# Windowed attention and its feed-forward layer: a lower place in the schedule for the weights' conversion passes while attention runs alone

## The chip, the cores and the metric

The kernel runs on one core of one Trainium2 chip. The metric is the device time in microseconds (us) of one execution, as the median of several runs. In the text PE is the matrix engine, DVE the vector engine, ACT the scalar engine, POOL the general-purpose engine, and SP the engine whose queue issues nearly all DMA transfers. Each engine works through a queue of its own in order: an instruction whose input is late holds up everything behind it in that queue.

## What is computed

Attention over 8 batches and 8 heads of width 64, with 32 global and 512 local positions; a local query sees the 32 global keys and the local keys within 32 positions. Its output, 4352 rows of 512 numbers, goes through two matrix products with an ELU between them.

```python
s_ll = np.where(np.abs(pos[:, None] - pos[None, :]) <= 32, scale * q_l @ k_l.T, -1e9)
out_l = sm(concat([scale * q_l @ k_g.T, s_ll])) @ concat([v_g, v_l])
out_g = sm(scale * q_g @ concat([k_g, k_l]).T) @ concat([v_g, v_l])
x = concat([out_g, out_l]).transpose(0, 2, 1, 3).reshape(8 * 544, 512)
h = x @ w_in                                   # w_in: 512 x 2048, float64 in the inputs
g = np.where(h > 0, h, np.exp(np.minimum(h, 0)) - 1)
out = g @ w_out                                # w_out: 2048 x 512, float64 in the inputs
```

## The kernel before

**The weights.** `w_in` and `w_out` arrive as 8-byte floats, are loaded as pairs of 32-bit integers, and have to become two float16 tensors each, a high and a low part. This is done in 16 units, alternately of `w_in` (m = 0) and `w_out` (m = 1), each a tile of 128 x 1024 elements. One unit is a chain of steps:

- `s0`: absolute value on ACT (L188) and a clamp on POOL (L189).
- `s1a`, `s1b`, `s1c`: three integer passes on DVE (L193, L196, L200) that put a 32-bit float together; L196 and L200 read two tiles.
- `s1d`: the largest magnitude, on DVE (L205) for m = 0 and on ACT (L207) for m = 1.
- `s2`: for m = 0 a transpose on PE (L141) and a reduction on DVE (L142), so that all partitions know the maximum.
- `s3`: three one-column operations on DVE (L131, L132, L136) and the high part on ACT (L216).
- `s4`: the low part on DVE (L219), which also reads two tiles.

Two tiles `raw` hold the loaded integers, three tiles `cu` the work. The DMA that loads the next unit but one therefore waits on SP until the last reader of its `raw` tile (L200 or L207) is done.

**Attention.** It goes through slots, each of four steps of the outer loop; in the stretch that matters here a slot is one tile of 128 queries for four heads, or the global queries of four heads. `stage_s` multiplies queries by keys on PE (L772) and masks and takes the minimum on DVE (L783); `ex` is the exponential on ACT (L789); `norm` takes the sum's reciprocal on DVE (L793, L794), scales on POOL (L796) and on DVE (L798). `stage_t` transposes on PE (L812) and copies on DVE (L814); `stage_u` transposes the global parts on PE (L745 to L748) and copies them on ACT (L749, L751, L753) and, for one tile in four, on DVE (L756). `stage_v` multiplies by the values on PE (L856, L825), copies on ACT (L862), and adds up on DVE (L867 to L871). `stage_ga` does the global queries (PE L706, DVE L718, L719, ACT L723). Transposes of a tile come two slots after its scores, its product with the values three slots after.

**The order.** Two things set it. The program issues instructions in an order that the Python loops fix: `defer(n, fn)` puts a step n ticks later, and one tick passes for each attention step while attention runs alone, which it does for its first 66 steps (`lead[0]` is true). Units 0 to 4 begin at steps 1, 8, 18, 30 and 64. From step 66 on the feed-forward layer's matmuls (L327, L450, later L485) are issued between attention's steps and fill PE. The second thing is a scheduler that runs at compile time: it goes through all instructions, estimates when each has its inputs, and gives each engine, of those that it takes to be ready, the one with the lowest number. The number is the place in the program's order. `tc.high_priority(offset=-BEHIND)`, with BEHIND = 60, gives what is issued inside it a number higher by 60. What the scheduler has put in a queue stays so on the chip, whatever is ready first there. `tc.keep_in_program_order` (on L193 and on the transposes of L141) pins an instruction behind the one that the program issued before it on the same engine, and says nothing of those after.

The kernel has a function `behind` for this already, inside `add_up`, which prepares sums of the weights after all are converted.

Of the kernel before, what the change touches and what calls it, by code (L numbers as in the profile page):

```python
# [44 lines left out]
BEHIND = 60  # L45
# [15 lines left out]
def attn_ffn(ctx: ExitStack, tc: tile.TileContext, qT, qgT, kT, vT, vgT, vpT, w_in, w_out, mask, out):  # L61
# [23 lines left out]
    def defer(n, fn):  # L85
        if n == 0:
            return fn()
        later.setdefault(now[0] + n, []).append(fn)

    def tick():  # L90
        now[0] += 1
        for fn in later.pop(now[0], []):
            fn()

    def drain():
        while later:
            tick()

    lead = [True]

# [27 lines left out]
    def power(dst, src):  # L128

        dst = dst.bitcast(I32)  # L130
        nc.vector.tensor_scalar(dst, src.bitcast(I32), 0x7f800000, None, ALU.bitwise_and)  # L131
        nc.vector.tensor_scalar_max(dst, dst, LOW)  # L132

    def inverse(dst, src):

        nc.vector.tensor_scalar(dst.bitcast(I32), src.bitcast(I32), TOP, -1.0, ALU.subtract, ALU.mult)  # L136

    def all_max(dst, src):

        tp = ps_a.tile([P, 512], F32, name="pa")  # L140
        tc.keep_in_program_order(nc.tensor.transpose(tp[:, 0:P], src.to_broadcast([P, P]), ident))  # L141
        nc.vector.tensor_reduce(out=dst, in_=tp[:, 0:P], op=ALU.max, axis=AX.X)  # L142
# [15 lines left out]
    def load_weights():  # L158
        todo = [(group, m, p) for group in "abcd" for p in range(*GROUPS[group]) for m in range(2)]
        raws = [fetch(*todo[0][1:])]  # L160
        yield
        for n, (group, m, p) in enumerate(todo):
            if n + 1 < len(todo):
                raws.append(fetch(*todo[n + 1][1:]))
            unit(m, p, raws[n])
            if (m, p) == (1, GROUPS[group][1] - 1):
                defer(12, lambda group=group: tables(group))
                if p == NP - 1:
                    defer(13, lambda: tables("f"))
            yield  # L170
# [6 lines left out]
    def unit(m, p, raw):  # L177
        f = slice(2 * p * P, 2 * (p + 1) * P)
        shape = [P, NC, 2 * P] if m == 0 else [P, 2, DM]
        parts = [w[:, :, f] for w in win] if m == 0 else [w[:, 2 * p:2 * p + 2, :] for w in wout]  # L180
        pw = (pww if m == 0 else pwo)[:, p:p + 1]
        u = ffn.tile(shape, F32, name="cu", bufs=3)
        mx = ffn.tile([P, 4], F32, name="cm", bufs=4)
        high, low = raw[..., 1], raw[..., 0]
        ui = u.bitcast(I32)

        def s0():
            nc.scalar.activation(u, high.bitcast(F32), AF.Abs)  # L188
            nc.gpsimd.tensor_scalar(u, u, FMAX, FMIN, ALU.min, ALU.max)  # L189

        def s1a():
            tc.keep_in_program_order(
                nc.vector.tensor_scalar(ui, ui, 3, 0x3ffffff8, ALU.logical_shift_left, ALU.bitwise_and))  # L193

        def s1b():
            nc.vector.scalar_tensor_tensor(out=ui, in0=high, scalar=-0x40000000, in1=ui,  # L196
                                           op0=ALU.bitwise_and, op1=ALU.bitwise_or)

        def s1c():
            nc.vector.scalar_tensor_tensor(out=ui, in0=low, scalar=29, in1=ui,  # L200
                                           op0=ALU.logical_shift_right, op1=ALU.bitwise_or)

        def s1d():
            if m == 0:
                nc.vector.tensor_reduce(out=mx[:, 0:1], in_=u, op=ALU.max, axis=AX.XY, apply_absolute_value=True)  # L205
            else:
                nc.scalar.activation(low.bitcast(F32), u, AF.Abs, accum_out=mx[:, 1:2])  # L207

        def s2():
            if m == 0:  # L210
                all_max(mx[:, 1:2], mx[:, 0:1])

        def s3():
            power(pw, mx[:, 1:2])
            inverse(mx[:, 3:4], pw)
            nc.scalar.activation(parts[0], u, AF.Copy, scale=mx[:, 3:4])  # L216

        def s4():
            nc.vector.scalar_tensor_tensor(out=parts[1].rearrange("p a b -> p (a b)") if m else parts[1],  # L219
                                           in0=u.rearrange("p a b -> p (a b)") if m else u, scalar=mx[:, 3:4],  # L220
                                           in1=parts[0].rearrange("p a b -> p (a b)") if m else parts[0],
                                           op0=ALU.mult, op1=ALU.subtract)

        d = 1 if lead[0] else 2
        lag = 7 if m else 16
        for i, fn in ((1, s0), (1 + d, s1a), (1 + 2 * d, s1b), (1 + 3 * d, s1c), (1 + 4 * d, s1d),
                      (1 + lag, s2), (2 + lag, s3), (3 + lag, s4)):
            defer(i, fn)

    def tables(group):  # L230

# [30 lines left out]
    def add_up(p, cross):  # L262


        if not sums:
            sums["rows"] = [ffn.tile([P, NP * 512], F16, name="raw") for _ in range(2)]
            sums["diag"] = [ffn.tile([P, NP * 256], F16, name="cu", bufs=3) for _ in range(2)]
        w = ffn.tile([P, 2, DM], F32, name="cu", bufs=3)
        s = ffn.tile([P, 512], F32, name="tmp", bufs=3)
        d = None if cross else ffn.tile([P, 512], F32, name="tmp", bufs=3)[:, 0:256]  # L270
        pr = slice(2 * p, 2 * p + 2)
        flat = [a[:, pr, :].rearrange("p a b -> p (a b)")[:, 256:768] for a in wout]
        rows = [a[:, p * 512:(p + 1) * 512] for a in sums["rows"]]
        diag = [a[:, p * 256:(p + 1) * 256] for a in sums["diag"]]
        todo = ((flat, s),) if cross else ((rows, s), (diag, d))

        def s0():
            nc.vector.tensor_add(w, wout[0][:, pr, :], wout[1][:, pr, :])  # L278

        def s1():  # L280
            if cross:
                nc.vector.tensor_sub(s, w[:, 1, :], w[:, 0, :])
            else:
                nc.vector.tensor_add(s.rearrange("p (a b) -> p a b", a=2), w[:, :, 0:256], w[:, :, 256:512])
                nc.vector.tensor_add(d, w[:, 0, 0:256], w[:, 1, 256:512])

        def s2():
            for dst, src in todo:
                nc.scalar.copy(dst[0], src)

        def s3():
            for dst, src in todo:
                nc.vector.tensor_sub(dst[1], src, dst[0])
            if cross:
                added.append(p)

        def behind(fn):
            with tc.high_priority(offset=-BEHIND):
                fn()

        for i, fn in enumerate((s0, s1, s2, s3)):
            defer(1 + 2 * i, lambda fn=fn: behind(fn))
# [6 lines left out]
    def ffn_stream():  # L309
# [288 lines left out]
        def load():  # L598
            if "f" in tab:
                n = state.setdefault("sums", 0)  # L600
                state["turn"] = not state.get("turn")
                if n < NP and state["turn"]:
                    add_up(n, False)
                    state["sums"] += 1
                n = state.setdefault("cross", 0)
                first = min((GROUPS["abcd"[step[b]]][0] for b in order if 0 < step[b] < 4), default=NP)
                if n < state["sums"] and not uses[n] and n < first:
                    add_up(n, True)
                    state["cross"] += 1
            for blk in order:  # L610
                if blk in ready and blk not in xs and not step[blk] and len(xs) < NX:
                    xs[blk] = split_x(blk)
# [409 lines left out]
    for _ in f:  # L1022
        tick()
    drain()


# [50 lines left out]
```

## Time and profile before

| | |
|---|---|
| median of 3 runs | 960.44 us (958.44 to 963.3) |
| the profiled execution's own time | 964.03 us |
| its span in the profile | 962.2 us |
| PE busy | 914.8 us (95%) |
| DVE, ACT, POOL busy | 738.6 us (77%), 661.9 us (69%), 273.1 us (28%) |
| first matmul of the feed-forward layer (L327) | 86.94 us from the span's start |

Rows of the profile have start, duration, engine, line, operation, output and inputs; square brackets show how long the engine stood idle before the instruction and what ended it. In the chain of work that ended last, each row is a piece of the path back from the last instruction, with the time that it holds on that path; "issue" is time in which an engine waited for nothing that the profile shows. Busy time by stretch gives, per engine, microseconds and the number of instructions, then the clock granted to PE (1.00 is full speed).

### The profile page before, as it was taken

How to read it: one execution, taken by the hardware profiler on the slowest of the kernel's cores; microseconds unless marked ns; L12 is line 12 of the kernel's file. 1: busy time of each engine (PE TensorE's matmuls, PEld its weight loads, DVE VectorE, ACT ScalarE, POOL GpSimd, SP SyncE). 2: the span in 40 equal slices, each digit the busy share in tenths (PEclk: the TensorE clock that was granted, in tenths of full speed). 3: DMA queues.
4: the chain of work that ended last, by engine and by line, in shares of the span. 5: the costliest groups of instructions: out<-in, count | busy, mean ns of one | idle time of the engine just before them, and what ended most of it. 6: DMA issues, size and time to landing. Idle time of an engine off the chain costs nothing.

```text
span 962.2 us, 23824 instructions
## 1 busy us (share of the span) xinstructions
PE 914.8 (95%) x9216; PEld 730.1 (76%) x9216; DVE 738.6 (77%) x2033; ACT 661.9 (69%) x1568; POOL 273.1 (28%) x483
## 2 busy tenths in 40 slices
PE   5887889899999999999999999999999999999997
PEld 2655566566666788788888888888888888888886
DVE  4877889989977876778776868687777877676566
ACT  4666788775676767757776866776776767666564
POOL 3636275372632212221221212222242222110000
PEclk7779899989999999999999999999999999999999
DMA  7852676622343114101230023001410101000000
GB/s 266 276 178 91 228 256 219 209 78 67 121 145 109 41 59 141 48 26 45 90 134 25 25 99 121 27 27 52 148 68 25 46 24 34 1 23 23 1 23 22
DMA packets 41769, 87.64 MB, mean 91 GB/s; under 512 B 7736, under 2 KB 8888, under 8 KB 41656
## 3 DMA queue, kind: packets, MB, share of 16 engines
q1 hardware_dynamic: 41368, 85.85, 26.4%
q8 instruction: 73, 1.20, 0.5%
q14 instruction: 40, 0.33, 0.1%
q10 hardware_dynamic: 288, 0.26, 0.1%
HBM read 70.89 MB, written 15.20 MB: 89 GB/s over the span
## 4 chain that ended last, share of the span: by engine, by line
PE 67%; DVE 17%; ACT 8%; issue 3%; POOL 3%; DMA 1%; DVEq 0%; SPq 0%; ACTq 0%; POOLq 0%
PE pa L327 25%; PE acc L485 12%; PE h L485 9%; PE pa L825 4%; PE acc L450 3%; PE pa L772 3%; PE h L327 3%; PE pa L812 2%; ACT p L789 2%; DVE gl L348 2%; PE pa L892 2%; DVE cu L278 1%; POOL p L796 1%; PE pa L706 1%; DVE cu L196 1%
## 5 line engine op out<-in xcount | busy, mean ns | idle before, releaser
L327 PEld LDWEIGHTS <-winh 128*128 128x128 f16 x2160 | 210.0, 99 | 42.0 <-issue 10.8
L796 POOL TENSOR_SCALAR p<-p,sm 128x128 f32<-128x128 f32 x256 | 144.1, 580 | 317.8 <-DVE sm L794 167.2
L327 PE MATMUL pa<-xh,winh 128*128 128x256 f16 x824 | 224.9, 273 | 0.1
L327 PE MATMUL pa<-xh,winl 128*128 128x256 f16 x824 | 224.6, 273 | 0.0
L327 PE MATMUL pa<-xl,winh 128*128 128x256 f16 x824 | 224.6, 273 | 0.0
L364 ACT ACTIVATE gh<-gx,xs 128x896 f16<-128x896 f32 x103 | 107.3, 1042 | 123.2 <-DVE gx L361 123.1
L348 DVE SCALAR_TENSOR_TENSOR gl<-gx,xs,gh 128x896 f16<-128x896 f32 x103 | 119.5, 1160 | 60.0 <-ACT gh L364 59.1
L485 PEld LDWEIGHTS <-gh 128*128 128x128 f16 x1456 | 139.6, 98 | 24.0 <-issue 7.4
L789 ACT ACTIVATE p<-p,m 128x160 f32<-128x160 f32 x256 | 106.6, 420 | 42.9 <-DVE m L783 41.3
L327 PEld LDWEIGHTS <-winl 128*128 128x128 f16 x1080 | 106.4, 99 | 14.5 <-issue 1.2
L336 ACT ACTIVATE g<-pa,xs 128x512 f32<-128x512 f32 x103 | 70.4, 683 | 24.1 <-PE pa L327 23.4
L485 PE MATMUL acc<-wouth,gh 128*128 128x256 f16 x312 | 85.2, 273 | 0.0
L485 PE MATMUL acc<-woutl,gh 128*128 128x256 f16 x312 | 85.0, 273 | 0.0
L485 PE MATMUL acc<-wouth,gl 128*128 128x256 f16 x312 | 85.0, 273 | 0.0
L338 ACT ACTIVATE g<-g 128x512 f32<-128x512 f32 x135 | 85.0, 630 | 0.0
L485 PEld LDWEIGHTS <-gl 128*128 128x128 f16 x728 | 71.2, 98 | 9.2 <-DVE gl L348 1.0
L327 PE MATMUL h<-xh,winh 128*128 128x256 f16 x256 | 71.9, 282 | 4.1 <-ACT hs L337 3.1
L485 PE MATMUL h<-raw,gh 128*128 128x256 f16 x416 | 75.0, 273 | 0.0
L327 PE MATMUL h<-xl,winh 128*128 128x256 f16 x256 | 71.8, 281 | 0.7 <-DVE xl L574 0.7
L327 PE MATMUL h<-xh,winl 128*128 128x256 f16 x256 | 71.8, 281 | 0.0
L783 DVE CUSTOM_DVE_ANT_0 p<-pa,msk 128x160 f32<-128x160 f32 x228 | 61.0, 317 | 7.1 <-PE pa L772 5.3
L345 DVE SCALAR_TENSOR_TENSOR gx<-g,hs 128x512 f32<-128x512 f32 x51 | 35.9, 705 | 36.0 <-ACT g L338 35.7
(237 smaller groups left out, 2028.8 us busy)
## 6 DMA issues: line engine op xcount, KB each, us to landing
k<-kT SPq DMA_DIRECT2D x32, 640.0 KB, 5.1
v<-vT SPq DMA_DIRECT2D x64, 256.0 KB, 2.7
q<-qT SPq DMA_DIRECT2D x32, 256.0 KB, 5.6
raw<-w_in SPq DMA_DIRECT2D x8, 1024.0 KB, 6.4
raw<-w_out SPq DMA_DIRECT2D x8, 1024.0 KB, 5.5
out<-o SPq DMA_DIRECT2D x32, 256.0 KB, 2.3
od<-o SPq DMA_DIRECT2D x24, 256.0 KB, 3.3
o<-od SPq DMA_DIRECT2D x24, 256.0 KB, 2.8
```

Of the source, the lines that this page charges most:

```text
L327: nc.tensor.matmul(h[:, j, :], wt[:, c, f], xt[:, c, :], start=k == 0, stop=k == 11)
L336: nc.scalar.activation(g, hf, AF.Relu, scale=sc[:, p:p + 1])
L338: nc.scalar.activation(g, g, AF.Exp, scale=-1.0)
L345: nc.vector.scalar_tensor_tensor(out=out, in0=ins[0], scalar=-1.0, in1=ins[1], op0=ALU.add, op1=ALU.max)
L348: nc.vector.scalar_tensor_tensor(out=dst, in0=src, scalar=sg, in1=hi, op0=ALU.mult, op1=ALU.subtract)
L364: nc.scalar.activation(gh, gx, AF.Copy, scale=sg)
L450: nc.tensor.matmul(acc[t], gt[:, s], wt[:, f, :], start=p == first and j == 0 and k == 0, stop=p == last and j == 1 and k == 2)
L485: nc.tensor.matmul(cols, gt, w, start=p == 0 and k == 0, stop=last and k == len(todo) - 1, skip_group_check=True)
L783: nc.vector.tensor_tensor_reduce(out=p, in0=sp[r][:, j * KW:(j + 1) * KW], in1=msk[:, mi, :], op0=ALU.add, op1=ALU.min, scale=-scale, scal ...
L789: nc.scalar.activation(ps[i], ps[i], AF.Exp, bias=m[:, i:i + 1], scale=-1.0, accum_out=s[:, 0, i:i + 1])
L796: nc.gpsimd.tensor_scalar(ps[i][:, 0:P], ps[i][:, 0:P], s[:, 1, i:i + 1], 1.0, ALU.mult, ALU.mult)
L825: nc.tensor.matmul(o[:, HQ * i:HQ * i + 96], v[:, 4 * i + h, :], x, start=False, stop=i == 1, skip_group_check=True)
```

## The change

The function `behind` moves to the outer scope, and for units that begin while `lead[0]` is true (units 0 to 4) every step but `s0` and `s2` is issued inside it. These steps (L193, L196, L200, L205 or L207, then L131 to L136, L216, L219) get a number higher by 60. No instruction is added or removed, the program's order, the pins and the buffers stay, and units 5 to 15 are issued as before.

```diff
+    def behind(fn):
+        with tc.high_priority(offset=-BEHIND):
+            fn()
...
         for i, fn in ((1, s0), (1 + d, s1a), (1 + 2 * d, s1b), (1 + 3 * d, s1c), (1 + 4 * d, s1d),
                       (1 + lag, s2), (2 + lag, s3), (3 + lag, s4)):
-            defer(i, fn)
+            defer(i, (lambda fn=fn: behind(fn)) if lead[0] and fn not in (s0, s2) else fn)
...
-        def behind(fn):
-            with tc.high_priority(offset=-BEHIND):
-                fn()
-
         for i, fn in enumerate((s0, s1, s2, s3)):
             defer(1 + 2 * i, lambda fn=fn: behind(fn))
```

## The prediction

> **What bounds the kernel now.** I read the page first, then busy time by stretch, then the groups of the first stretch, and last the chain of waits and the queues in order of time. Three lines of the page: the span, PE's share, and the shares of the chain that ended last.
>
> ```profile
> span 962.2 us, 23824 instructions
> PE 914.8 (95%) x9216; PEld 730.1 (76%) x9216; DVE 738.6 (77%) x2033; ACT 661.9 (69%) x1568; POOL 273.1 (28%) x483
> PE 67%; DVE 17%; ACT 8%; issue 3%; POOL 3%; DMA 1%; DVEq 0%; SPq 0%; ACTq 0%; POOLq 0%
> ```
>
> PE is the bound on the whole, but only two thirds of the chain are PE; DVE holds 17%. Where, the stretches tell. The columns are the stretch, its length, busy time and count on PE, weight loads, DVE, ACT and POOL, the clock, DMA share and GB/s.
>
> ```profile
> 0.00:87.00 87.00, 63.44 (x631) 40.54 (x632) 62.81 (x256) 53.44 (x185) 45.72 (x101) 0.80 0.61 209
> 87.00:962.00 875.00, 851.32 (x8587) 689.53 (x8585) 675.76 (x1778) 608.45 (x1383) 227.34 (x383) 0.99 0.24 79
> 100.00:260.00 160.00, 147.16 (x1178) 96.98 (x1175) 151.00 (x346) 122.83 (x263) 75.59 (x99) 0.95 0.51 170
> 14.00:31.05 17.05, 10.21 (x78) 6.64 (x78) 12.99 (x34) 10.56 (x34) 8.92 (x16) 0.50 0.72 255
> ```
>
> In the first 87 us, before the feed-forward matmuls begin, PE is idle for 87.00 - 63.44 = 23.6 us and its clock averages 0.80: no engine is full, attention's chain of small steps sets the pace. In the 875 us behind it PE idles as long (23.7 us). So what the first stretch loses or gains moves all that follows, one to one, unless the crowded part (DVE 151.00 of 160.00 us between 100 and 260) orders itself anew. The change can act in the first stretch alone, and for unit 4 just behind it.
>
> What the moved steps cost there, by groups up to 87 us (DVE, then ACT; count, then busy time and mean):
>
> ```profile
> L200 DVE SCALAR_TENSOR_TENSOR cu<-raw,cu 128x1024 int32<-128x1024 int32 x4 | 4.9, 1226 | 0.0
> L196 DVE SCALAR_TENSOR_TENSOR cu<-raw,cu 128x1024 int32<-128x1024 int32 x4 | 4.9, 1226 | 0.0
> L193 DVE TENSOR_SCALAR cu<-cu 128x1024 int32<-128x1024 int32 x5 | 3.5, 701 | 2.9 <-POOL cu L189 2.9
> L219 DVE SCALAR_TENSOR_TENSOR winl<-cu,cm,winh 128x1024 f16<-128x1024 f32 x2 | 2.7, 1332 | 2.1 <-ACT winh L216 2.1
> L219 DVE SCALAR_TENSOR_TENSOR woutl<-cu,cm,wouth 128x1024 f16<-128x1024 f32 x2 | 2.6, 1276 | 0.0
> L205 DVE TENSOR_REDUCE cm<-cu 128x1 f32<-128x1024 f32 x2 | 2.4, 1202 | 0.0
> L207 ACT ACTIVATE raw<-cu 128x1024 f32<-128x1024 f32 x2 | 2.3, 1152 | 5.0 <-DVE cu L200 5.0
> L216 ACT ACTIVATE winh<-cu,cm 128x1024 f16<-128x1024 f32 x2 | 2.3, 1142 | 0.0
> L216 ACT ACTIVATE wouth<-cu,cm 128x1024 f16<-128x1024 f32 x2 | 2.3, 1140 | 0.1
> ```
>
> DVE spends 21.0 us and ACT 6.9 us on them. None of it goes away. What can go is the time for which these long passes (1.1 to 1.3 us, against 0.3 us for most of attention's) stand in front of an attention step that is ready. The chain shows which do:
>
> ```profile
> 19.27 1.22 DVE cu L196
> 20.80 1.14 DVE cu L200
> 22.46 1.21 DVE cm L205
> 23.67 1.13 DVE cu L196
> 24.89 0.19 DVE ptg L756
> 25.12 0.80 PE h L856 x4
> 28.14 0.87 PE pa L812 x4
> ...
> 29.72 1.19 DVE woutl L219
> 33.37 0.78 DVE cu L193
> 34.15 1.30 DVE winl L219
> 35.45 0.14 DVE mg L719
> ...
> 58.06 1.11 ACT raw L207 x2
> 59.17 1.04 ACT winh L216
> ```
>
> The moved passes hold 1.22 + 1.14 + 1.21 + 1.13 + 1.19 + 0.78 + 1.30 + 1.11 + 1.04 = 10.1 us of this chain. That is the gross gain, if each of them left it and nothing else were late.
>
> **The change part by part.** An offset of 60 instructions is about one slot of attention, as the code has it: 8 matmuls and 4 masks in S, 4 exponentials, 7 instructions of `norm`, 5 of T, 5 to 7 of U, 28 of V. A pass falls behind an attention step only when the program issues that step less than 60 instructions after it, and when the scheduler takes the step to be ready. I count place by place.
>
> *First place, 19 to 25 us.* These rows are of PE, DVE and POOL in order of time.
>
> ```profile
> 25.12 0.80 PE L856 MATMUL h<-ptg,ptw 128*64 128x160 f32 x4 [5.23 <-DVE ptg L756]
> 20.40 0.16 DVE L793 TENSOR_SCALAR sm<-sm 128x4 f32<-128x4 f32 x1
> 24.72 0.17 DVE L794 RECIPROCAL sm<-sm 128x4 f32<-128x4 f32 x1
> 24.98 4.05 POOL L796 TENSOR_SCALAR p<-p,sm 128x128 f32<-128x128 f32 x8 [5.76 <-DVE sm L794]
> 33.10 3.90 POOL L796 TENSOR_SCALAR p<-p,sm 128x128 f32<-128x128 f32 x4 [0.69 <-DVE sm L794]
> 49.71 2.99 POOL L796 TENSOR_SCALAR p<-p,sm 128x128 f32<-128x128 f32 x4 [1.85 <-DVE cm L142]
> 54.18 1.52 POOL L796 TENSOR_SCALAR p<-p,sm 128x128 f32<-128x128 f32 x4 [1.48 <-DVE sm L794]
> ```
>
> PE stands 5.23 us for L756, a DVE step of 0.19 us, with four long passes in front of it; POOL waits 5.76 us for L794, whose partner L793 ran 4.3 us before. The program issues L756 at step 15. Between the passes L200 and L205 of unit 0 (steps 5 and 6) and it lie some 70 instructions, so these two stay ahead, and so does unit 0's L196. Unit 1's L193 and L196 (steps 10 and 11) lie about 40 before it and fall behind. L756 gains 0.70 (mean of L193) + 1.13 = 1.8 us. L794 belongs to step 12 and passes in front of all of them, but its POOL work is not what PE waits for here. Bounds: 0, if the scheduler takes L756 to be ready late, and 4.7, if all four passes fall behind. I take 1.8.
>
> *Second place, 29 to 39 us.* L719 (step 20) has L219 of units 1 and 0 and unit 2's L193 in front of it on the chain, all issued within 60 instructions before it or later: 1.19 + 0.78 + 1.30 = 3.3 us. Late next is POOL's L796: it begins at 33.10 and takes 3.90 us, where an undisturbed four take 1.52 (54.18). If the passes no longer run beside it, it ends 3.90 - 1.52 = 2.4 us earlier and its start moves up by some tenths, as POOL's L189 stands before it; if they still do, only the tenths remain. Between 0.7 and 3.1 us I take the middle, 2.0.
>
> *Third place, 58 to 60 us.* L207 (step 35) and L216 stand on ACT before four exponentials that the program issues at steps 38 and 39, about 60 instructions on. This can fall either way: between 0 and 2.15 I take half, 1.1.
>
> *The clock.* From 14.00 to 31.05 us PE has half its clock (row above). PE's work on the chain from 25.12 to the end of L812 at 29.01 is 3.9 us; at full clock half of it, 1.9 us, would go. The gap of 5.23 us ahead of it shrinks by the 1.8. Between 0 and 1.9 I take 0.9. The Trainium skill ("TensorE: Matmul & The Clock Gate", "Why this matters for your kernels") asks for no PE gaps longer than about 3 us, because one idle window brings the half clock back. By it the remaining gap of 3.4 us is borderline, and the sum would be between 0.9 us less and 1.0 us more than mine. No run so far shows which.
>
> *Unit 4*, whose passes run between 85 and 94 us, where the feed-forward work begins. These rows are a DVE row, two of the chain, and ACT.
>
> ```profile
> 88.66 1.21 DVE L200 SCALAR_TENSOR_TENSOR cu<-raw,cu 128x1024 int32<-128x1024 int32 x1
> 90.50 1.08 POOL p L796 x3
> 91.69 7.54 DMA raw<-w_in
> 99.24 1.14 ACT L188 ACTIVATE cu<-raw 128x1024 f32<-128x1024 f32 x1 [1.13 <-DMA raw<-w_in]
> ```
>
> L200 frees the `raw` tile at 89.87, SP issues its next load at 91.69, and ACT waits for that load 1.13 us with feed-forward steps queued behind. L200 may thus run 1.8 us later before the load does. Falling behind L756 and L793 costs it some tenths, so 0; if the cover is gone, each further microsecond is one for ACT. In the lead itself a later L200 or L207 holds SP's loads of values and queries queued behind the `raw` load; no wait of attention for such a load stands on the chain there, so 0, with 1 us as the upper bound. The moved functions issue no DMA.
>
> *Sum.* 1.8 + 2.0 + 1.1 + 0.9 = 5.8 us. The profiled execution of 964.03 us would become 958.2. It lies 3.6 us above the median of 960.44, so in medians the forecast is 954.7. The most would be the 10.1 gross and 1.9 of clock: 948.4.
>
> **The rivals.** *The queues hardly change.* The scheduler only prefers among steps that it takes to be ready. At 17 us DVE stood 2.9 us for L189 with L193 at the head of its queue (the L193 group): its estimate and the chip differ. If it believes attention's inputs late where on the chip they are there, the passes keep their places. Then 960.4, give or take 2. Against it: L794 was put 4.3 us behind L793, with passes between, which has the look of a preference.
>
> *POOL pays.* Passes that run when attention leaves DVE free run just when POOL scales with L796, since that is what attention then waits for. In the rows above L796 takes 3.90 and 2.99 us beside passes, and 4.05 for eight, against 1.52 for four: an excess of 2.4 + 1.5 + 1.0 = 4.9 us now. Three passes (L193, L219, L196) ran beside the first, 0.8 us of excess each. Twelve passes with two inputs (L196, L200, L219, four each) stand before 87 us; if every one held an L796 for its whole 1.22 us, the excess would be 14.7, 9.8 more than now. Against the 5.8 this is 4.0 us slower than before: 964.4. It turns into a loss once L796 exceeds its undisturbed time by more than 4.9 + 5.8 = 10.7 us up to 87 us. Against it: POOL's wait begins earlier too, and nothing makes all twelve meet an L796. The Trainium skill ("SBUF — State Buffer", "Who interferes with whom") says the same of the pair of ports that DVE and POOL share: a DVE instruction with two inputs in SBUF and a POOL instruction that reads SBUF exclude each other for the whole of the one that began. The 3.90 us row agrees.
>
> *The crowded part orders itself anew.* Everything behind 87 us is planned from a new start. Its 23.7 us of idle PE come in a few waits; a changed order there may add or take some 6 us, a quarter. Added, with no gain ahead that survives it, that is 966; taken, 949.
>
> **How the numbers follow.** Half a per cent, 4.8 us, is about what a measurement of this kernel tells from no change, as the three runs spread by that. The forecast with its bounds gets 0.50, of which 0.40 lie beyond 0.5%; unchanged queues 0.22; POOL 0.13, about half of it beyond 0.5% slower; the new order 0.15, of which 0.12 slower and 0.03 faster. Faster 0.43, within 0.5% 0.38, slower 0.19. The forecast's own range is 948 to 959; with POOL's 964.4 and the 966 of the new order the range is 948 to 966.
>
> **What would show it.** Right: PE's wait for L756 falls from 5.23 to about 3.4 us, L794 follows L793 at once, the two L196 of the first units no longer both stand before L756, L719 runs about 3 us earlier against PE's start of the second tiles, and the first L327 comes near 81 us instead of 86.94, with everything later moved as much. Wrong: L327 comes early and the end doesn't (the new order), L796 rows between 3 and 5 us for four in most slots (POOL), the same sequence on DVE up to 40 us (unchanged queues), or ACT's wait for the `raw` load near 94 us above 3 us (unit 4).

## The result, and the profile after

Over eleven runs of each the kernel before takes 960.44 us in the median and the changed kernel 954.00: a ratio of 0.9936, with a 95% interval of 0.9914 to 0.9958. That is 6.4 us less by medians; means of the runs (960.7 and 955.1) differ by 5.6. The forecast in medians was 954.7. In what follows, lines 99 to 295 of the kernel before stand four lines later in the changed one (L193 has become L197, L196 L200, L200 L204, L205 L209, L207 L211, L216 L220, L219 L223, and the POOL clamp L189 L193); later lines keep their numbers.

The page of the changed kernel, the lines that answer to the first three shown before:

```profile
span 950.9 us, 23813 instructions
PE 906.4 (95%) x9216; PEld 727.0 (76%) x9216; DVE 736.6 (77%) x2033; ACT 661.8 (70%) x1568; POOL 280.3 (29%) x483
PE 68%; DVE 17%; ACT 8%; POOL 3%; issue 3%; DMA 1%; DVEq 0%; ACTq 0%; POOLq 0%; SPq 0%
```

The counts of the four engines are the same, and the shares of the chain are within one point of those before: nothing shows at this level but the span, 11.3 us shorter. Where it went, busy time by stretch tells, cut at the first L327 (79.34 us; it was at 86.94):

```profile
0.00:79.34 79.34, 58.06 (x631) 39.02 (x631) 60.41 (x255) 53.66 (x184) 48.66 (x99) 0.83 0.67 229
79.34:950.90 871.56, 848.31 (x8588) 688.01 (x8585) 676.18 (x1779) 608.12 (x1385) 231.64 (x385) 0.99 0.24 80
```

Of the 11.3 us, 7.6 were won ahead of the first L327 and 3.7 behind it. That split is luckier than the change. The profiled execution of before lay 3.6 us above its median and that of the changed kernel 1.2 below, and a second profiled pair gives less. Here are the first L856, the first L327 and the stretch behind it, first of the second execution of before, then of the second of the changed kernel:

```profile
24.60 0.80 PE L856 MATMUL h<-ptg,ptw 128*64 128x160 f32 x4 [5.23 <-DVE ptg L756]
82.88 0.37 PE L327 MATMUL h<-xh,winh 128*128 128x256 f16 x1
82.88:956.80 873.92, 848.91 (x8588) 687.42 (x8585) 677.25 (x1779) 608.28 (x1385) 228.33 (x385) 0.99 0.24 79
```

```profile
22.43 0.80 PE L856 MATMUL h<-ptg,ptw 128*64 128x160 f32 x4 [2.66 <-DVE ptg L756]
80.40 0.27 PE L327 MATMUL h<-xh,winh 128*128 128x256 f16 x1
80.40:951.90 871.50, 848.14 (x8588) 687.84 (x8585) 676.56 (x1779) 608.53 (x1383) 229.39 (x384) 0.99 0.24 80
```

The first L327 comes 7.6 us earlier in one pair and 2.5 in the other, 5.0 in the mean. PE's wait for L756 is 5.23 us in both executions of before and 2.66 in both after. The waits belong to the program, while part of the rest belongs to the execution.

What the changed order looks like on DVE between 19 and 30 us (changed kernel; the rows of the steps named here, in order of time, with others between them left out):

```profile
19.03 0.16 DVE L793 TENSOR_SCALAR sm<-sm 128x4 f32<-128x4 f32 x1
19.09 1.22 DVE L200 SCALAR_TENSOR_TENSOR cu<-raw,cu 128x1024 int32<-128x1024 int32 x1
20.23 0.17 DVE L794 RECIPROCAL sm<-sm 128x4 f32<-128x4 f32 x1
20.74 1.31 DVE L204 SCALAR_TENSOR_TENSOR cu<-raw,cu 128x1024 int32<-128x1024 int32 x1
21.97 0.28 DVE L756 TENSOR_REDUCE ptg<-pa 128x32 f32<-128x128 f32 x1
22.17 1.20 DVE L209 TENSOR_REDUCE cm<-cu 128x1 f32<-128x1024 f32 x1
23.70 0.66 DVE L197 TENSOR_SCALAR cu<-cu 128x1024 int32<-128x1024 int32 x1
24.97 1.22 DVE L200 SCALAR_TENSOR_TENSOR cu<-raw,cu 128x1024 int32<-128x1024 int32 x1
...
29.52 0.20 DVE L719 TENSOR_SCALAR mg<-mg 128x1 f32<-128x1 f32 x1
```

Two long passes of unit 0 still stand ahead of L756, which starts at 21.97 us (before: 24.80). Unit 0's maximum L209, unit 1's L197 and its L200 now stand behind it. L794, the reciprocal, follows L793 by 1.2 us instead of 4.3, with one pass between. L719 runs at 29.52 instead of 35.37.

### The profile page after: what moved, and what is told of

It is laid out like the page before. It is cut to its first block, busy times and chain, and to the rows that moved or that the text cites. A ratio compares the mean times of both kernels' runs of the same rounds, so it can differ in the third digit from the quotient of the medians.

```text
span 950.9 us, 23813 instructions
## 1 busy us (share of the span) xinstructions
PE 906.4 (95%) x9216; PEld 727.0 (76%) x9216; DVE 736.6 (77%) x2033; ACT 661.8 (70%) x1568; POOL 280.3 (29%) x483
## 4 chain that ended last, share of the span: by engine, by line
PE 68%; DVE 17%; ACT 8%; POOL 3%; issue 3%; DMA 1%; DVEq 0%; ACTq 0%; POOLq 0%; SPq 0%
PE pa L327 25%; PE acc L485 12%; PE h L485 9%; PE pa L825 4%; PE pa L772 3%; PE acc L450 3%; PE h L327 3%; PE pa L812 3%; ACT p L789 2%; DVE gl L348 2%; PE pa L892 2%; DVE cu L282 1%; PE pa L706 1%; DVE cu L204 1%; DVE p L783 1%
## 5 line engine op out<-in xcount | busy, mean ns | idle before, releaser
L327 PEld LDWEIGHTS <-winh 128*128 128x128 f16 x2160 | 209.6, 98 | 42.0 <-issue 11.0
L796 POOL TENSOR_SCALAR p<-p,sm 128x128 f32<-128x128 f32 x256 | 143.2, 575 | 306.8 <-DVE sm L794 154.1
L327 PE MATMUL pa<-xh,winh 128*128 128x256 f16 x824 | 224.9, 273 | 0.1
L327 PE MATMUL pa<-xh,winl 128*128 128x256 f16 x824 | 224.6, 273 | 0.0
L327 PE MATMUL pa<-xl,winh 128*128 128x256 f16 x824 | 224.6, 273 | 0.0
L327 PEld LDWEIGHTS <-winl 128*128 128x128 f16 x1080 | 106.2, 98 | 14.3 <-issue 1.2
L327 PE MATMUL h<-xh,winh 128*128 128x256 f16 x256 | 71.3, 280 | 4.4 <-ACT hs L337 3.4
L327 PE MATMUL h<-xl,winh 128*128 128x256 f16 x256 | 71.5, 280 | 0.7 <-DVE xl L574 0.7
L327 PE MATMUL h<-xh,winl 128*128 128x256 f16 x256 | 71.7, 280 | 0.0
```

What stands on the lines that cost most here:

```text
L327: nc.tensor.matmul(h[:, j, :], wt[:, c, f], xt[:, c, :], start=k == 0, stop=k == 11)
L796: nc.gpsimd.tensor_scalar(ps[i][:, 0:P], ps[i][:, 0:P], s[:, 1, i:i + 1], 1.0, ALU.mult, ALU.mult)
```

## The experiments

Four explanations went into them. *Order*: attention's short steps overtake long passes in DVE's queue, and PE and POOL get their inputs sooner. *Clock*: the shorter gap on PE spares it time at half clock, and that is the gain. *New plan*: everything behind the first L327 is planned anew, and the gain, or a loss, lies there. *POOL pays*: passes moved into attention's pauses hold up POOL. Ratios are to the kernel before, run in turn with the variant on the same chip, with 6 to 12 runs of each variant. The kernel before took 960.86, 959.75 and 962.46 us in the median in the three groups of runs, so the ratios compare variants and the medians do not.

**The clock alone.** The order stays that of before; ten matmuls over zeros (128 x 512) are issued into PE's gap ahead of L756, after the fourth tile's scores.

```diff
+    def fill(): a = ps_o.tile([P, DM], F32, name="acc"); [tc.keep_in_program_order(nc.tensor.matmul(a, warm[:, 0:P], warm, start=True, stop=True)) for _ in range(10)]
...
+            fill() if np_[0] in (12,) else None; mi = 0 if t == 0 else (2 if t == NT - 1 else 1)
```

> Ten idle matmuls on a block of zeros (128x512, 0.43 us each at half clock) go into the kernel before, into PE's gap of 5.23 us ahead of the first product with the values; nothing moves on DVE, ACT and POOL. Order theory (the gain is that attention's steps pass the conversion passes in their queues): the first L327 stays within 1 us of 86.9 us and the time within 2 us of 960. Clock theory (the gain is that the shorter gap gives PE its full clock back sooner): the half clock that lasted from 14.0 to 31.05 us ends some 7 us sooner, the first L327 comes 2 us or more earlier, the time falls to 957 or below.

Measured: ratio 0.9997 (0.9978 to 1.0016), 960.77 us. Rows of PE and a stretch of this kernel, the last number but two of the stretch being the clock:

```profile
19.65 4.04 PE L100 MATMUL acc<-wouth 128*128 128x512 f16 x10
24.95 0.49 PE L856 MATMUL h<-ptg,ptw 128*64 128x160 f32 x4 [1.26 <-DVE ptg L756]
12.90:23.10 10.20, 7.65 (x32) 3.58 (x33) 6.37 (x16) 6.89 (x25) 5.58 (x11) 0.50 0.58 216
```

The gap was filled, and the half clock ended at 23.1 us instead of 31.05 (28.40 in the second execution of before). The mean clock over the runs rose too, to 0.979 from 0.975. The first L327 came at 82.13 us, which the clock theory had named as its sign; but it came at 82.88 in the second execution of before, without any fill, so the sign tells nothing. The time did not move: L856 still began at 24.95, since it had DVE to wait for. The interval leaves room for a gain of 0.22%, and the change gains 0.42% or more by its own. So the clock in this gap is not the cause of the gain.

**The two halves of the change.** Only the passes (L193 to L207 of before) behind attention; then only the tails (L131 to L136, L216, L219):

```diff
-            defer(i, (lambda fn=fn: behind(fn)) if lead[0] and fn not in (s0, s2) else fn)
+            defer(i, (lambda fn=fn: behind(fn)) if lead[0] and fn in (s1a, s1b, s1c, s1d) else fn)
```

> Only s1a to s1d (the three integer passes and the maximum) get the lower place, s3 and s4 not. Order theory: PE's wait for L756 is near 2.7 us as in the changed kernel, the two low-part passes stand before L719 again and take back some 2.5 us, so the first L327 comes near 82 us and the time near 956. New-plan theory (the gain comes from how the rest happens to be arranged): no relation to the places, anything between 953 and 963.

```diff
+            defer(i, (lambda fn=fn: behind(fn)) if lead[0] and fn in (s3, s4) else fn)
```

> Only s3 and s4 (the scale, the high and the low part) get the lower place. Order theory: PE's wait for L756 stays at 5.2 us, L719 comes some 2.5 us earlier than in the kernel before, the first L327 near 84 us, the time near 958. New-plan theory: anything between 953 and 963.

Measured: the passes alone 0.9946 (0.9926 to 0.9966), 954.99 us; the tails alone 0.9995 (0.9979 to 1.0012), 959.33. The tails were expected to bring something and brought nothing that can be told from none, although they pulled L719 forward. Rows of the kernel with the passes alone (PE and DVE), and then of the one with the tails alone:

```profile
22.19 0.80 PE L856 MATMUL h<-ptg,ptw 128*64 128x160 f32 x4 [2.66 <-DVE ptg L756]
30.33 0.67 DVE L814 COPY ptw<-pa 128x512 f32<-128x512 f32 x1
30.93 1.96 DVE L223 SCALAR_TENSOR_TENSOR woutl<-cu,cm,wouth 128x1024 f16<-128x1024 f32 x1
32.80 1.27 DVE L223 SCALAR_TENSOR_TENSOR winl<-cu,cm,winh 128x1024 f16<-128x1024 f32 x1
34.00 0.20 DVE L719 TENSOR_SCALAR mg<-mg 128x1 f32<-128x1 f32 x1
```

```profile
25.15 0.80 PE L856 MATMUL h<-ptg,ptw 128*64 128x160 f32 x4 [5.23 <-DVE ptg L756]
32.05 0.20 DVE L719 TENSOR_SCALAR mg<-mg 128x1 f32<-128x1 f32 x1
36.70 0.68 DVE L814 COPY ptw<-pa 128x512 f32<-128x512 f32 x1
```

With the passes alone L719 comes at 34.00, behind both low parts L223: 1.4 us earlier than before, 4.5 later than in the whole change. Yet the third tile's copy L862 starts at 35.41 us, even before the 36.83 of the whole change, and well before the 42.44 of the kernel before. With the tails alone L719 comes at 32.05, that copy only at 40.39, and PE still waits 5.23 us for L756. So an early L719 is neither needed for an early third tile nor enough for it. The third tile's L814, which is in both fences, does go with it; the section on the prediction comes back to it.

**How far behind.** The offset, BEHIND = 60 in the change, as 30 and, in another kernel with 120 in the last line, as 120, for these steps alone.

```diff
-    def behind(fn):
-        with tc.high_priority(offset=-BEHIND):
+    def behind(fn, n=BEHIND):
+        with tc.high_priority(offset=-n):
             fn()
...
-            defer(i, (lambda fn=fn: behind(fn)) if lead[0] and fn not in (s0, s2) else fn)
+            defer(i, (lambda fn=fn: behind(fn, 30)) if lead[0] and fn not in (s0, s2) else fn)
```

> The offset is 30 instead of 60 for the same steps. Counted from the program's order, L193 and L196 of unit 1 lie about 40 instructions before L756, so with 30 they stay ahead of it. Order theory: PE's wait for L756 is 4.5 us or more, the first L327 comes at 84 us or later, the time is 957 or more. Theory that any lower place does it: like the changed kernel, L327 near 79 us and 954.

> The offset is 120 instead of 60. Order theory: the passes of unit 0 fall behind more steps of attention too (L794 and the masks of the fourth tile), PE's wait for L756 shrinks to 2 us or less; later the weights of the first group are ready some us later, which matters only if the first L327 waits for them, and it has 40 us in hand; the time 950 to 955. Theory that the passes lie in the way wherever they are put (DVE is 70% busy): no better than 60, 954 to 957.

Measured: 30 gives 0.9977 (0.9957 to 0.9996), 957.06 us; 120 gives 0.9950 (0.9931 to 0.9969), 955.17. The first L856 at 30; then, at 120, the DVE pass ahead of L756 and the first L856:

```profile
25.00 0.80 PE L856 MATMUL h<-ptg,ptw 128*64 128x160 f32 x4 [5.51 <-DVE ptg L756]
```

```profile
21.23 1.25 DVE L200 SCALAR_TENSOR_TENSOR cu<-raw,cu 128x1024 int32<-128x1024 int32 x1
22.74 0.80 PE L856 MATMUL h<-ptg,ptw 128*64 128x160 f32 x4 [2.79 <-DVE ptg L756]
```

At 30 PE's wait is as long as before and about a third of the gain is left; the first L327 came at 82.66 us, where 84 or later was expected. At 120 the wait is that of 60, not the 2 us or less that was expected: unit 0's other pass L204 did fall behind L756, but L200 stays directly ahead of it, with more of attention's masks in front. A higher number didn't move it, which fits a scheduler that took L756's input to be late there; that reading was not tested by itself.

**Which units.** The two that begin at steps 1 and 8 (p = 0); the three after them (p > 0); unit 4 alone (p = 2).

```diff
+            defer(i, (lambda fn=fn: behind(fn)) if lead[0] and p == 0 and fn not in (s0, s2) else fn)
```

> Only units 0 and 1 get the lower place (units 2, 3 and 4 as before). Order theory: PE's wait for L756 is 2.7 us as in the changed kernel, the gain of the first place (some 2.8 us) and part of the second remain, the first L327 comes near 82 to 83 us, the time near 957. Theory that later units carry it: time within 2 us of 960.

> Only units 2, 3 and 4 get the lower place. Order theory: PE's wait for L756 stays 5.2 us, what is gained lies behind 30 us (L193 of unit 2 before L719, the passes of unit 3 before L794), some 2 us, the time near 958. With the run of units 0 and 1 the two gains should add up to some 6 us, if they are of places; if the plan as a whole makes it, they need not.

> Only unit 4 gets the lower place; its passes run where the feed-forward matmuls begin. Order theory of the lead: nothing before 85 us changes, the time stays within 2 us of 960. Theory that part of the gain is made where unit 4 meets the feed-forward work: 955 to 957, with the first L327 within 1 us of the kernel before.

Measured: units 0 and 1 0.9974 (0.9958 to 0.9991), 957.55 us; units 2 to 4 0.9940 (0.9917 to 0.9963), 954.16; unit 4 alone 0.9982 (0.9963 to 1.0000), 960.33. PE's wait for L756 is 2.66 us in the first, 5.23 in the others. The middle one is a miss: it was expected at 958, since I had counted most of the gain in the first two units. (Its profiled execution took 958.84, the longest of its eight runs.) The two parts sum to 0.26% + 0.60% = 0.86%, against 0.64% for the whole, which the intervals allow. By these figures the later units, which begin at step 18 and beyond, carry no less than the first two, and the prediction's places do not say why. One step that unit 2's passes hold up, the third tile's L814, is shown further down; how much of the gain it carries stays open. What part of it is unit 4's is open between nothing and 0.37%.

**The clamp as well, and all units.** `s0` (the clamp on POOL) put behind as well; then the change without `lead[0]`, for all sixteen units.

```diff
+            defer(i, (lambda fn=fn: behind(fn)) if lead[0] and fn is not s2 else fn)
```

> s0 (absolute value on ACT, clamp on POOL) gets the lower place as well. Order theory: the clamp no longer splits the four L796 of the first tile (1.04 us at 15.85 us of the changed kernel) and the absolute value no longer the exponentials (1.0 us at 13.18 us), so PE's first L812 to L856 come up to 2 us earlier, time 952 to 954. Rival: s0 starts each unit's chain, so its delay moves the three passes into later steps and the `raw` loads with them: time 954 to 958.

```diff
+            defer(i, (lambda fn=fn: behind(fn)) if fn not in (s0, s2) else fn)
```

> All 16 units get the lower place, also those that run beside the feed-forward layer, where DVE is busy for 94% of the time. Order theory: attention's and the feed-forward steps pass the passes there as well, but DVE has no free time to make up for it, so the conversion falls behind: 952 to 957. Rival: the weights of the later groups come too late and PE waits, 960 or more.

Measured: with the clamp 0.9969 (0.9949 to 0.9989), 956.24 us; all units 0.9918 (0.9890 to 0.9946), 953.72, not to be told from the change. DVE and PE of the kernel with the clamp:

```profile
20.21 1.52 DVE L197 TENSOR_SCALAR cu<-cu 128x1024 int32<-128x1024 int32 x1 [0.88 <-POOL cu L193]
...
23.10 0.28 DVE L756 TENSOR_REDUCE ptg<-pa 128x32 f32<-128x128 f32 x1
23.43 0.80 PE L856 MATMUL h<-ptg,ptw 128*64 128x160 f32 x4 [5.08 <-DVE ptg L756]
```

The late clamp holds DVE's queue at L197 for 0.88 us, and L756 comes 1.1 us later than in the change. PE's wait is 5.08 us again, though L856 still begins 1.7 us earlier than before: PE is done with the work ahead of the wait at 18.35 us instead of 19.89, since the clamp no longer splits the first tile's L796. Leaving `s0` in its place, as the change does, has the better ratio, but the two intervals overlap.

**Both kernels once more**, one more profiled execution of each, to see what belongs to the program and what to the execution; their rows stand in the section on the result.

> The kernel before, for a second profiled execution. If the clock's half-speed stretches differ between executions of one kernel, the first L327 comes 2 us or more away from 86.94 us, with the same order in all queues; if not, within 0.5 us.

> The changed kernel, for a second profiled execution: the first L327 between 79 and 82 us, in the same order of the queues; the stretch behind it 871 to 876 us, by its half-clock time.

Measured: the first L327 at 82.88 us in the kernel before, 4.1 us from the first execution, with the same order on DVE and ACT, and at 80.40 in the changed kernel, with 871.5 us behind it.

Single profiles rank nothing here. The kernel with units 0 and 1 has its first L327 at 79.69 us and takes 957.55 in the median; the one with units 2 to 4 has it at 81.73 and takes 954.16. Each is one execution with its own stretches of half clock, so the verdicts above rest on the ratios alone, and the rows only on which instruction waits for which.

## Why the prediction was right, and where it was not

*The first place was mis-sized.* It was put at 1.8 us; L856 came 2.8 and 2.2 us earlier in the two pairs, and PE's wait fell by 2.6. The step that failed is "these two stay ahead": L205 (now L209) lies some 70 instructions before L756, as the prediction has it, but fell behind it, as did unit 1's two. What stayed ahead is unit 0's L196 and L200. Its number alone would have kept L205 ahead (70 is more than 60); it reads the tile that L200 has just written, so that the scheduler took it to be not yet ready there would fit, but was not tested. The direction and the mechanism were right, and the bound of 4.7 us held.

*The second place had about the right size, by a wrong route.* The third tile's copy L862 starts at 42.44 us before and at 36.83 in the changed kernel. It gained 5.6 us (4.5 in the second pair, from 41.72 to 37.27), so 2.8 and 2.3 beside the first place's, where 2.0 were put. The prediction derived this from L719 and POOL's L796. DVE's queue shows a nearer step: L814, which copies the third tile's transposes into the tile that its product with the values (L825) reads. The transposes on PE and then DVE, before; then L814 in the changed kernel:

```profile
31.23 0.66 PE L812 MATMUL pa<-ident,p 128*128 128x128 f32 x4
33.37 0.78 DVE L193 TENSOR_SCALAR cu<-cu 128x1024 int32<-128x1024 int32 x1
34.07 1.38 DVE L219 SCALAR_TENSOR_TENSOR winl<-cu,cm,winh 128x1024 f16<-128x1024 f32 x1
35.50 1.26 DVE L196 SCALAR_TENSOR_TENSOR cu<-raw,cu 128x1024 int32<-128x1024 int32 x1
36.81 1.26 DVE L200 SCALAR_TENSOR_TENSOR cu<-raw,cu 128x1024 int32<-128x1024 int32 x1
38.45 0.67 DVE L814 COPY ptw<-pa 128x512 f32<-128x512 f32 x1
```

```profile
29.77 0.68 DVE L814 COPY ptw<-pa 128x512 f32<-128x512 f32 x1
```

Before, the transposes are done at 31.9 us, and L814 comes at 38.45, behind 4.7 us of moved passes: three of unit 2 and the low part of unit 0. In the changed kernel these passes come later than L814. This is the mechanism of the prediction at a step that it did not count. The chain of before went by L719 because PE's queue was late as well: at 38.73 it had waited 1.13 us for L753, which stood on ACT behind the exponentials L723 that need L719.

Over all fourteen profiled executions, the third tile's L814 starts at 36.7 to 38.5 us in the kernel before and in the three variants without a clear gain (fill, tails, unit 4), and at 29.6 to 34.3 in all others. Units 2 to 4 alone bring it to 34.31. But no run moved L814 alone, and the gains do not follow its time in size (34.31 us goes with a ratio of 0.9940, 29.60 with the 0.9974 of units 0 and 1). That it is the route of the second place fits these rows and is not shown.

The reciprocal L794 and POOL's scaling behind it, which the prediction had set aside as "not what PE waits for here", moved ahead too. Groups of POOL up to the first L327, before and then changed:

```profile
L796 POOL TENSOR_SCALAR p<-p,sm 128x128 f32<-128x128 f32 x47 | 24.4, 538 | 20.7 <-DVE sm L794 18.7 <-DVE cm L142 1.9
L734 POOL TENSOR_SCALAR pk<-pu,sg 32x32 f32<-32x32 f32 x16 | 4.6, 288 | 12.7 <-ACT p L789 9.3 <-DVE sg L731 2.4
```

```profile
L796 POOL TENSOR_SCALAR p<-p,sm 128x128 f32<-128x128 f32 x45 | 21.0, 484 | 13.2 <-DVE sm L794 8.4 <-ACT ptw L749 4.2 <-PE pa L812 0.2
L734 POOL TENSOR_SCALAR pk<-pu,sg 32x32 f32<-32x32 f32 x16 | 8.9, 559 | 13.6 <-ACT p L789 9.1 <-DVE wm_b L240 3.1 <-DVE sg L731 0.5
```

POOL's idle time ahead of L796 for want of L794 fell from 18.7 to 8.4 us, and PE's waits for L796 up to 90 us from 8.6 to 5.9. No run took the earlier L794 away by itself, so what it is worth stays open.

*The third place gave nothing* of its 1.1 us. These rows are of the changed kernel's chain:

```profile
55.43 1.14 ACT raw L211 x2
56.56 1.05 ACT winh L220
57.64 1.29 DVE winl L223
```

Both ACT passes still stand on the chain, now followed by the low part L223. "This can fall either way" fell to zero. Behind it part of the gain is given back. By the copies L862 of successive tiles the first pair's lead grows from 4.2 to 8.0 us and falls to 6.4; the second's grows to 5.1 and falls to 2.4, between about 60 and 70 us. There L571 and L574, steps of the attention output's own conversion with an ordinary preference, stand on the chain of the changed kernel (at 66.33 and 67.41 us); the change does not touch them. Part of the second pair's loss is a load: in the second execution of the changed kernel ACT waits 1.40 us for a `raw` load until 64.50 us, and in the first it does not. The rest of the difference between the pairs stays open.

*The clock's 0.9 us was not seen.* Two stretches of equal length at half clock, in the second execution of before and in the changed kernel:

```profile
14.70:28.40 13.70, 8.08 (x53) 5.78 (x54) 10.67 (x29) 7.20 (x26) 7.68 (x14) 0.50 0.68 242
```

```profile
13.50:27.20 13.70, 9.17 (x62) 6.32 (x66) 10.01 (x28) 8.46 (x32) 10.87 (x17) 0.50 0.66 237
```

PE's clock stays at half for 13.7 us whether the gap within is 5.23 us or 2.66. Over all fourteen profiled executions this first stretch lasts 13.7 us in the six with a gap of 2.66 to 2.79 us, 13.7 in five and 17.1 in two of those with 5.08 to 5.51, and 10.2 with the gap filled, so a small effect of the gap is not excluded. Over all runs the mean clock is 0.9753 before (77 runs) and 0.9761 after (11): 2 x 0.0247 x 960 = 47.4 us at half clock against 2 x 0.0239 x 955 = 45.6, so 1.8 us less, worth 0.9 us if all of it lay on the path; so small a difference cannot be told from none here: the three groups of runs of before alone have means of 0.9742 to 0.9759. The prediction's sentence from the Trainium skill ("TensorE: Matmul & The Clock Gate", "Why this matters for your kernels"), that gaps over about 3 us bring the half clock back, made a gap near that length decide over some 2 us. The two rows do not show that: the clock was at half before either gap began, and came back after the same time.

*The sum* of 5.8 us met 6.4 by medians and 5.0 ahead of the first L327: two places at 2.5 us each, as means of the two pairs, where 1.8 and 2.0 were put, and two terms, 1.1 and 0.9, at nothing that could be seen. So the closeness of the total is in part luck: two terms too small and two too large cancel.

*"One to one" held.* Behind the first L327 the four executions took 875.3 and 873.9 us before and 871.6 and 871.5 after. What differs there is mostly half clock. The first execution of before, for one, has 22.0 us at half clock there, and 875.3 less half of that is 864.3. Taking away half of the half-clock time in the same way leaves 864.3 to 867.6 us in all fourteen profiled executions, variants included. The *new order* did not show as a gain or a loss.

*POOL did pay, elsewhere than foreseen.* Its busy time up to the first L327 rose from 45.66 to 48.66 us, although L796 fell by 3.4 (with 45 of them instead of 47 in the stretch, at 484 ns instead of 538). The groups above show L734 nearly doubled. POOL and DVE rows of before and then of the changed kernel:

```profile
39.29 1.37 POOL L734 TENSOR_SCALAR pk<-pu,sg 32x32 f32<-32x32 f32 x4 [0.20 <-DVE sg L731]
39.12 1.19 DVE L205 TENSOR_REDUCE cm<-cu 128x1 f32<-128x1024 f32 x1
```

```profile
32.53 3.65 POOL L734 TENSOR_SCALAR pk<-pu,sg 32x32 f32<-32x32 f32 x4 [0.52 <-DVE sg L731]
33.11 1.31 DVE L223 SCALAR_TENSOR_TENSOR woutl<-cu,cm,wouth 128x1024 f16<-128x1024 f32 x1
34.35 1.30 DVE L223 SCALAR_TENSOR_TENSOR winl<-cu,cm,winh 128x1024 f16<-128x1024 f32 x1
```

Beside L205, which reads one tile, four L734 take 1.37 us; beside two L223, which read two each, 3.65, that is 2.3 us more beside 2.6 us of passes. The trace agrees with the Trainium skill ("SBUF — State Buffer", "Who interferes with whom"): DVE's second SBUF input shuts POOL's reads out for the whole instruction. L796, which PE does wait for, took less in sum and not more, so the rival's point of 10.7 us was never near.

*Unit 4* cost nothing, as put: where ACT waited 1.13 us for the next `raw` load before, it does not wait in the changed kernel (L192 at 93.57 us). The second execution of before has no wait there either, so its going is not to the credit of the change.

## What to carry to other kernels

In an in-order queue, look for the short step that another engine is waiting for and count the long, patient passes placed ahead of it: 10.1 us of such passes on the chain were worth about 6 us here, without any work removed. Give the lower preference to the long passes alone and try a few offsets, since too small a one leaves the wait in place and a larger one than needed adds nothing; leave out the step that feeds the same queue, or it can be late for its own consumer. A pass that stands on the chain need not be the only one that sets the time, since another step may be nearly as late: undo it alone before you credit it.

## What the runs showed of the hardware beyond expectation

The time at half clock differs between executions of one program: the mean clock up to the first L327 was 0.80 in one of before and 0.86 in the other, so 2 x 0.20 x 86.94 = 35 us and 2 x 0.14 x 82.88 = 23 us at half clock, with the same order on DVE and ACT and the same 5.23 us wait. Of eleven runs of the changed kernel, the three slowest (958.8 to 959.1 us) have a mean clock of 0.972 and the others (952.4 to 955.4) 0.975 to 0.979. So here a difference of 4 us between two single executions says nothing. Half clock removed where PE waits for DVE anyway bought nothing that could be measured, as the filled gap shows.

The stretches at half clock shown here last 17.05, 13.70, 13.70 and 10.20 us, close to 5, 4, 4 and 3 times 3.41. The Trainium skill ("TensorE: Matmul & The Clock Gate", "What's actually happening") gives the clock gate a window of 3413 ns that runs freely, whatever the kernel does. These lengths agree, and a phase that differs from one execution to the next would fit the spread above; no run here sets that phase, so it is not shown.
